# Attention beside linear attention on one core: a planner's fixed rules replaced by a table of rules per short stretch, and the last output rows summed ahead

## The chip, the cores and the metric

The kernel runs on one core of one Trainium2 chip. The metric is the device time of one execution in microseconds (us); a kernel's time is the median over its runs. Engines are named as the profile names them: PE (TensorE, matmuls), PEld (its weight loads), DVE (VectorE), ACT (ScalarE), POOL (GpSimd), SP (SyncE, which issues most of the DMAs).

## What is computed

Two independent blocks, each on an input of 2048 rows by 512 columns in bfloat16, with 32 heads of 16 columns. Their outputs stand side by side in the result.

```python
# A: linear attention
phi = lambda t: jnp.where(t > 0, t + 1, jnp.exp(t)) + 1e-6
pq, pk = phi(q), phi(k)
kv = jnp.einsum("bhsd,bhse->bhde", pk, v)
z = jnp.einsum("bhsd->bhd", pk)
num = jnp.einsum("bhqd,bhde->bhqe", pq, kv)
den = jnp.einsum("bhqd,bhd->bhq", pq, z)[..., None] + 1e-6
a = (num / den).transpose(...).reshape(B, S, D) @ wo
# B: full softmax attention
scores = jnp.einsum("bhqd,bhkd->bhqk", q, k) * Dh ** -0.5
p = softmax(scores, axis=-1)
b = jnp.einsum("bhqk,bhkd->bhqd", p, v).transpose(...).reshape(B, S, D) @ wo
out = jnp.concatenate([a, b], axis=-1)
```

B has 32 x 2048 x 2048 scores, so 134 million exponentials; A is small beside it.

## The kernel before, in words

**Tiling of B.** The heads go in four groups of eight (`Gp`), a group in two halves of four heads (`e_`), the queries in four chunks of 512 (`c`). One unit is one group, one chunk and one half: 32 units, each with 16 key tiles for each of 4 heads, so 64 blocks. A block is 128 keys by 512 queries of one head; there are 2048 of them. The four heads of a unit sit in four row strips of PE (32 rows each) when scores are made, and in four column strips (17 columns: 16 of V and one of ones, which sums the row) when probabilities are multiplied with V, so up to four blocks run side by side.

**Two ways through the exponential.** A block's scores (line 727, `qk`) go either into the PSUM tile `pS`, or into one of the two banks of `pD`.

- The ACT way: `pS` has two slots, of three banks and of two. When a slot is filled (`fill_act_cand`), ACT takes the exponential of all its blocks in one instruction (line 896, 128x1536 or 128x1024) and writes `PT`. One PV matmul per block follows (line 971, `pPV<-PT`).
- The DVE and POOL way: DVE turns one bank of scores into 16-bit integers whose bits are a power of two (line 808, `DI<-pD`), and POOL adds two shifts to a pair of such blocks (line 832), which gives three approximations that are summed with three scaled copies of V. So three PV matmuls per block follow (`pPV<-DI`). `fill_d_cand` and `d_pick` decide which block goes this way and when.

After a unit's last PV matmul `unit_done` (line 987) transposes `pPV` on DVE (line 991), takes the reciprocal of the row sums on DVE (996), multiplies on POOL (997), and after the second half transposes the result into `ON` on DVE (1002). In the last group each finished chunk yields four output jobs (`omm_job`, line 671): four matmuls with Wo (line 675), an eviction (450) and a store (679). Block A is cut into jobs too (K, V, their sum, Q, denominators, numerators, output), which use the banks of `pD`.

**What sets the order.** Nothing is written out by hand. When the program is built, a planner runs through the work with its own clock for each engine and, step by step, picks the next instruction among the candidates: a fill of a `pS` slot, a block for `pD`, one to three rounds of PV matmuls (`pv_cand`), a stage of a job. Each candidate has a start time and a priority, and of those that could start within 0.03 us of the earliest the best priority is taken. `lim` is the planner's latest time at which PE must be free for the next fill of a slot; longer candidates are put off. Constants steer it: `DEFER` and `FLOW` (how early a fill is urgent), `DPR` and `DDEL` (priority and delay of a `pD` block), `PVR`, `PVMIN`, `PVURG` (rounds of PV, how many must be ready), `DBL` and `DLEAD` (how much work may queue on DVE and POOL), `DNEXT`, `ALAG`, `SLK`. Every engine then executes its own instructions strictly in the planned order, and waits on semaphores for the others. So a heavy row in PE's list delays every fill behind it.

`filler` (line 1115) puts idle matmuls into PE's planned gaps: into `pPV` with weights of zero (1125) or into a free bank of `pD` with the identity (1134). They change no result.

Of the kernel before, what the change touches and what calls it, by code (L numbers as in the profile page):

```python
# [231 lines left out]
def bass_concat_heads__linear_attn_block__softmax_full_mha__prompt_kernel(nc, A_x, A_wqkv, A_wo, B_x, B_wqkv, B_wo, out):  # L232
# [15 lines left out]
    DNEXT = 16  # L248
    DEND = 20
    TEND = 720.0  # L250
    ALAG = 10.0
    DLEAD = 1.0
    DBL = 3.0
    TRACE = None

# [6 lines left out]
    with es:  # L262
# [140 lines left out]
        class Job:  # L403
# [11 lines left out]
            def stage_done(self, i, end, bk, bi):  # L415
                if i == self.rel and bi is not None:
                    jfree[bi] = end + LAT
                for st, tk in self.gives:
                    if st == i:
                        tok[tk] = end + LAT  # L420
                if i + 1 < len(self.stages):
                    eng, dur, fn = self.stages[i + 1]
                    lat = LAT if eng != self.stages[i][0] else 0.0
                    push(eng, end + lat, self.prio if eng == "pe" else (0 if i + 1 <= self.rel and self.bank else min(self.prio, 2)), dur,
                         lambda st_, en_, fn=fn: (fn(bk), self.stage_done(i + 1, en_, bk, bi)), "PORT" in getattr(fn, "keys", ()))
# [11 lines left out]

        MM, TRB = 0.2155, 0.0555
# [4 lines left out]
        SLK = 0.0  # L443
        FMARG = 0.06
        DEFER, FLOW, DPR, DDEL = 0.15, 3.5, 4.2, 0
        PVR, PVMIN, PVURG = 3, 4, 32
# [237 lines left out]

        rem = [[list(range(NT)) for g in range(4)] for u in range(NU)]
# [30 lines left out]
        def take(bl, parts):  # L716
            for u, j, g in bl:
                rem[u][g].remove(j)
                pv_all[u][g] += parts
                left[u] -= 1  # L720
                if left[u] == 0 and (u + 1) % (NC * 2) == 0:
                    tok[("filled", u // (NC * 2))] = T["pe"]

# [38 lines left out]
        def d_pick(at, used):  # L762

            u = cur_unit()
            bi = min((i for i in range(2) if jfree[i] is not None), key=lambda i: (jfree[i], i), default=None)
            if bi is None or jfree[bi] > at or not d_open() or d_backlog(at) > DBL:
                return None
            if (ajobs and at > ajobs[0].ready + ALAG) or (bjobs and at > bjobs[0].ready + ALAG and bjobs[0].start_time() is not None):
                return None
            if u < NU - 1 and left[u] < DNEXT:  # L770
# [133 lines left out]
        def fill_d_cand():  # L904
            fr = [x for x in jfree[0:2] if x is not None]
            if not fr:
                return None
            busy = max(T["dve"], T["pe"]) + sum(c_[3] for c_ in cands["dve"] if c_[0] < T["dve"] + 1.0)
            at = max(T["pe"], min(fr), busy - DLEAD, T["pe"] + d_backlog(T["pe"]) - DBL + 0.01)
# [12 lines left out]
            return at, QK, run  # L922
# [4 lines left out]
        def pv_cand(lim, short):  # L927
# [20 lines left out]
            for R in range(1, PVR + 1):  # L948
# [7 lines left out]
            if n < (PVMIN if lim is not None else 4) and not final and not (short and n >= 1):  # L956
                return None
# [27 lines left out]
            return t_, dur, run, (1 if out_ >= PVURG or final else 4)  # L985

        def unit_done(u, t_):
# [7 lines left out]
            zr = ZR[:, 0, 0:16]  # L995
            st = [("dve", 0.25, f_op("dve", lambda e: e.reciprocal(zr, o[:, :, 16]), [("OT", 0)], [("ZR", 0)])),  # L996
                  ("pool", 0.65, f_op("pool", lambda e: e.tensor_tensor(xn[:, :, 16 * e_:16 * e_ + 16], o[:, :, 0:16],  # L997
# [77 lines left out]
        def job_cand():  # L1075
# [7 lines left out]
            for lst, pr in ((urgent, 0.5), (early, 2), (bjobs, 2.2), (urgent2, 2.3), (ajobs, 2.5)):  # L1083
                for pos, j_ in enumerate(lst[:1] if lst is not urgent2 else lst[:8]):
# [9 lines left out]
                    if best is None or (st, pr) < (best[0], best[1]):  # L1094
                        def run(st_, en_, j_=j_, lst=lst, fn=fn):
# [4 lines left out]
                            fn(bk)  # L1100
                            j_.stage_done(0, en_, bk, b_)
                        best = (st, pr, eng, dur, run)
# [41 lines left out]
        npick = 0  # L1144
        while True:
            opts = []
            for eng in T:
# [6 lines left out]
                if best is not None:  # L1154
                    c_ = best[2]
                    opts.append(pe_opt(best[1], c_[1], c_[3], c_[4], c_, "f") if eng == "pe" else (best[1], c_[1], eng, c_[3], c_[4], c_))
            fa = fill_act_cand()
            if fa is not None:
                lim = max(T["act"] + sum(exps) - fa[1] - PH - LAT - SLK, fa[0]) if nfill[0] >= 2 else None
                have = sum(x is not None and x <= fa[0] + 0.05 for x in jfree[0:2])  # L1160
                want = min(2, 4 - ABL[nfill[0] % 2])
                fao = pe_opt(fa[0], 0 if lim is None or fa[0] + DEFER > lim or have >= want or not d_open() else FLOW, fa[1], fa[2], None, "q")
                opts.append(fao)
            fd = fill_d_cand()
            if fd is not None:
                opts.append(pe_opt(fd[0] + DDEL, DPR, fd[1], fd[2], None, "q"))
            elif not d_open():
                close_group()
            if fa is None or nfill[0] < 2:
                lim = None  # L1170
            pc = pv_cand(lim, fa is None and not cands["act"])
            if pc is not None:
                opts.append(pe_opt(pc[0], pc[3], pc[1], pc[2], None, "v"))
            jc = job_cand()
            if jc is not None:
                opts.append(pe_opt(jc[0], jc[1], jc[3], jc[4], None, "f") if jc[2] == "pe" else (jc[0], jc[1], jc[2], jc[3], jc[4], None))
# [3 lines left out]
            if lim is not None:  # L1180
                keep = [o for o in opts if o[2] != "pe" or o is fao or o[0] + o[3] <= lim or o[0] + 1e-9 < fa[0] - o[3]]
                opts = keep
            t0 = min(o[0] for o in opts)
            o = min((o for o in opts if o[0] <= t0 + 0.03), key=lambda o: (o[1], o[0]))
# [99 lines left out]
```

## Time and profile before

| what | value |
|---|---|
| time, median of 3 runs | 738.66 us (735.14 to 738.72) |
| the profiled execution | 740.72 us, of which 738.8 us lie between its first and last instruction (the span) |
| granted TensorE clock, mean | 0.988 |
| instructions | 15635 |
| weight loads (PEld) | 229.5 us busy |
| bytes moved | 17.33 MB, most of it in the first 37 us |
| last exponential ends, span ends | 723.57 us, 738.8 us |

In the profile's rows a group gives its busy time and the mean length of one instruction; where instructions of an engine overlap, the mean is longer than the distance from one to the next. In rows of waits and in square brackets of a timeline, the engine and line behind the arrow is what ended the idle time. Granted clock 1.00 is full speed, 0.50 half.

### The profile page before, as it was taken

How to read it: one execution, taken by the hardware profiler on the slowest of the kernel's cores; microseconds unless marked ns; L12 is line 12 of the kernel's file. 1: busy time of each engine (PE TensorE's matmuls, PEld its weight loads, DVE VectorE, ACT ScalarE, POOL GpSimd, SP SyncE). 2: the span in 40 equal slices, each digit the busy share in tenths (PEclk: the TensorE clock that was granted, in tenths of full speed). 3: DMA queues.
4: the chain of work that ended last, by engine and by line, in shares of the span. 5: the costliest groups of instructions: out<-in, count | busy, mean ns of one | idle time of the engine just before them, and what ended most of it. 6: DMA issues, size and time to landing. Idle time of an engine off the chain costs nothing.

```text
span 738.8 us, 15635 instructions
## 1 busy us (share of the span) xinstructions
PE 694.7 (94%) x6677; PEld 229.5 (31%) x6677; DVE 519.3 (70%) x918; ACT 704.7 (95%) x657; POOL 535.0 (72%) x325
## 2 busy tenths in 40 slices
PE   7999999999999999999999999999999999999986
PEld 4333433333333333322222232222222222222221
DVE  5878656576666776678786778867777767776751
ACT  6899999898999999999999999999999999989992
POOL 4596446566876776767898869867788867879780
PEclk9999999999999999999999999999999989999998
DMA  9800000000000000100100000000100001010001
GB/s 212 216 2 2 2 1 10 8 12 5 1 2 1 2 1 2 36 8 12 34 16 15 2 8 23 24 19 11 23 16 23 8 17 28 22 44 8 30 1 32
DMA packets 35788, 17.33 MB, mean 23 GB/s; under 512 B 26496, under 2 KB 35200, under 8 KB 35712
## 3 DMA queue, kind: packets, MB, share of 16 engines
q1 hardware_dynamic: 34912, 15.87, 8.7%
q8 instruction: 54, 0.88, 0.5%
q10 hardware_dynamic: 800, 0.39, 0.2%
q14 instruction: 22, 0.18, 0.1%
HBM read 4.72 MB, written 4.19 MB: 12 GB/s over the span
## 4 chain that ended last, share of the span: by engine, by line
ACT 77%; PE 17%; DVE 2%; POOL 1%; DMA 1%; SPq 1%; issue 1%; DVEq 0%
ACT PT L896 75%; PE pPV L971 6%; PE pS L727 4%; ACT EA L586 2%; POOL DI L832 1%; PE pD L675 1%; PE pD L482 1%; DVE DI L808 1%; PE pD L566 1%; PE pD L597 1%; DMA xTb<-in_B_x_dram 1%; PE pD L727 1%; PE pD L1134 1%; SPq L344 1%; PE pD L622 0%
## 5 line engine op out<-in xcount | busy, mean ns | idle before, releaser
L896 ACT ACTIVATE PT<-pS 128x1536 f16<-128x1536 f32 x602 | 692.4, 1336 | 14.4 <-PE pD L727 11.1
L832 POOL TENSOR_TENSOR DI<-DI,SHC 128x1024 int32<-128x1024 int32 x272 | 509.7, 1891 | 174.2 <-DVE DI L808 148.0
L808 DVE TENSOR_SCALAR DI<-pD 128x512 int16<-128x512 f32 x539 | 359.8, 689 | 122.1 <-PE pD L727 114.2
L727 PE MATMUL pS<-QT,KM 32*128 32x512 bf16 x1504 | 235.3, 387 | 22.6 <-ACT PT L896 18.7
L971 PE MATMUL pPV<-PT,VV 128*17 128x512 f16 x1504 | 251.0, 386 | 1.1 <-ACT PT L896 0.8
L971 PE MATMUL pPV<-DI,VV 128*17 128x512 f16 x1632 | 243.5, 387 | 2.2 <-DVE OT L991 1.8
L727 PE MATMUL pD<-QT,KM 32*128 32x512 bf16 x544 | 194.6, 387 | 5.8 <-DVE DI L808 3.5
L727 PEld LDWEIGHTS pS<-QT,KM 32*128 32x128 bf16 x1504 | 57.2, 91 | 221.1 <-ACT PT L896 168.8
L971 PEld LDWEIGHTS pPV<-DI,VV 128*17 128x17 bf16 x1632 | 52.5, 88 | 75.3 <-issue 55.3
L971 PEld LDWEIGHTS pPV<-PT,VV 128*17 128x17 bf16 x1504 | 54.6, 88 | 61.9 <-issue 46.2
L727 PEld LDWEIGHTS pD<-QT,KM 32*128 32x128 bf16 x544 | 46.5, 91 | 58.3 <-DVE DI L808 31.2
L597 PE MATMUL pD<-Wa,xTa 128*128 128x128 bf16 x512 | 37.4, 220 | 1.0 <-DVE DI L808 0.6
L482 PE MATMUL pD<-xTb,Wb 128*128 128x512 bf16 x124 | 34.0, 384 | 0.9 <-DMA xTb<-in_B_x_dram 0.7
L991 DVE STREAM_TRANSPOSE OT<-pPV 128x512 f32<-128x512 f32 x32 | 22.8, 711 | 15.2 <-PE pPV L971 14.8
L597 PEld LDWEIGHTS pD<-Wa,xTa 128*128 128x128 bf16 x512 | 28.7, 98 | 14.3 <-DVE DI L808 7.3
L997 POOL TENSOR_TENSOR OT<-OT,ZR 128x256 bf16<-128x256 f32 x32 | 19.8, 620 | 16.3 <-DVE ZR L996 15.0
L586 ACT ACTIVATE EA<-pD 128x256 bf16<-128x256 f32 (+1 forms) x48 | 26.1, 544 | 0.0
L587 DVE TENSOR_SCALAR EA<-EA 128x256 bf16<-128x256 bf16 (+1 forms) x48 | 11.8, 245 | 18.5 <-POOL DI L832 8.4
L566 PE MATMUL pD<-Wb,xTb 128*128 128x128 bf16 x256 | 17.9, 220 | 1.8 <-DVE KM L495 0.7
L622 PE MATMUL pD<-xTa,Wa 128*128 128x512 bf16 x64 | 19.2, 398 | 0.1
L675 PE MATMUL pD<-WOa,ONT 128*128 128x512 bf16 x64 | 18.5, 383 | 0.1
L571 DVE CAST VV<-pD 128x512 bf16<-128x512 f32 x16 | 11.0, 689 | 8.2 <-PE pD L566 8.2
(89 smaller groups left out, 277.4 us busy)
## 6 DMA issues: line engine op xcount, KB each, us to landing
out_dram<-OB SPq DMA_DIRECT2D x16, 128.0 KB, 1.7
out_dram<-KNa SPq DMA_DIRECT2D x16, 128.0 KB, 1.8
Wa<-in_A_wqkv_dram SPq DMA_DIRECT2D x1, 1536.0 KB, 7.3
KM<-KR SPq DMA_DIRECT2D x96, 16.0 KB, 1.8
Wb<-in_B_wqkv_dram SPq DMA_DIRECT2D x2, 384.0 KB, 4.9
Wb<-in_B_wqkv_dram SPq DMA_DIRECT2D x1, 512.0 KB, 4.7
WOa<-in_A_wo_dram SPq DMA_DIRECT2D x1, 512.0 KB, 8.0
VNa<-in_B_wo_dram SPq DMA_DIRECT2D x1, 512.0 KB, 3.3
```

The costliest lines, as they stand in the source:

```text
L482: return e.matmul(f32v(bk), lhsT=Wb[:, cc, kind * 512 + Gp * 128:kind * 512 + Gp * 128 + 128], rhs=xTb[:, cc, sc * 512:(sc + 1) * 512], st ...
L566: return e.matmul(f32v(bk)[:, tl * 128:(tl + 1) * 128], lhsT=xTb[:, cc, t * 128:(t + 1) * 128], rhs=Wb[:, cc, 1024 + Gp * 128:1024 + Gp * ...
L586: ("act", 0.051 + n * 0.000833, f_ev("act", lambda e, bk: e.activation(EA[:, q, 0:n], f32v(bk)[:, c0:c0 + n], ACTF.Exp), [], [("EA", q)])),
L597: return e.matmul(f32v(bk)[:, 128 * x:128 * x + 128], lhsT=xTa[:, cc, (t + i_) * 128:(t + i_ + 1) * 128], rhs=Wa[:, cc, c0:c0 + 128], star ...
L675: return e.matmul(f32v(bk), lhsT=src, rhs=WO[:, hb, :], start=(hb == 0), stop=(hb == 3))
L727: return e.matmul(dst, lhsT=KM[32 * g:32 * g + 32, Gp % 2, e_, j * 128:(j + 1) * 128], rhs=QT[32 * g:32 * g + 32, Gp % 2, c * 512:(c + 1) ...
L808: sch.add("dve", lambda e: e.tensor_scalar(DI[:, buf, 0, i * 512:(i + n) * 512], DB[:, bi * 512:(bi + n) * 512], ESC, EB, op0=ALU.mult, op ...
L832: sch.add("pool", lambda e: e.tensor_tensor(DI32[:, buf, 1:3, 0:w], DI32[:, buf, 0, 0:w].unsqueeze(1).broadcast_to([128, 2, w]), SHC32[:]. ...
L896: sch.add("act", lambda e: e.activation(PT[:, row, c0:c0 + w], SCR[sl][:, 0:w], ACTF.Exp, scale=SC), reads=skeys(sl), writes=[("PT", row, ...
L971: sch.add("pe", lambda e, g=g, vk=vk, c0=c0, P=P, first=first, last_=last_: e.matmul(PVb[32 * g:32 * g + 17, 0:512], lhsT=VV[:, Gp % 2, vk ...
L991: sch.add("dve", lambda e: e.transpose(OT[:, 0, :], PVb[:, 0:512]), reads=[("PV", g) for g in range(4)], writes=[("OT", 0)])
L997: ("pool", 0.65, f_op("pool", lambda e: e.tensor_tensor(xn[:, :, 16 * e_:16 * e_ + 16], o[:, :, 0:16], zr.unsqueeze(2).broadcast_to([128, ...
```

## The change

**The rules come from a table.** The constants move into a table `POLICY` of 88 rows; row n holds while PE's planned clock is between 8n and 8(n+1) us, the last one to the end. A row has the old constants and four new numbers: `PA` and `PB` (added to the priority of PV and of jobs while the three-bank slot, or the two-bank slot, is next), `SEED` (a seed for random shifts of up to 0.7 in the priorities of PE's less urgent candidates) and `PARTS` (how many PE stages of one job may run in one piece, if they end before `lim`). `lim` is now also set while a slot is still held by its exponential. The rows were chosen by a search with the planner's own clock. In the diff the table is cut to two rows.

**The end.** Of the last four output row tiles, three of four Wo products are summed ahead (`pre_job`) once the last scores are filled; when the last chunk is finished one matmul per tile is left (`last_job`), and its eviction and store go to DVE and SP for two tiles, to ACT and ACT's own DMA queue for the other two. The multiply of the very last unit moves from POOL to DVE. After the last fill, `filler` uses half of a gap.

```diff
+    NAMES = ('DEFER', 'FLOW', 'DPR', 'DDEL', 'PVR', 'PVMIN', 'PVURG', 'DBL', 'DLEAD', 'DNEXT', 'ALAG', 'SLK', 'PA', 'PB', 'SEED', 'PARTS')
+    SEG = 8.0
+    POLICY = [
+        (0.15, 3.5, 4.2, 0, 3, 4, 32, 3.0, 1.0, 16, 10.0, 0.0, 0, 0, 0, 1),
...
+        (0.15, 3.5, 4.2, 0, 3, 4, 32, 3.0, 0.2, 16, 10.0, 0.0, 0, 0, 443, 2),
+    ]
...
-        DEFER, FLOW, DPR, DDEL = 0.15, 3.5, 4.2, 0
-        PVR, PVMIN, PVURG = 3, 4, 32
...
+        def pre_job(tl):
+            t = 12 + tl
+            def mm(bk):
+                prebank[tl] = bk
+                def f(e):
+                    for hb in range(3):
+                        ins = e.matmul(f32v(bk), lhsT=ON[:, 4 * hb + 3, tl * 128:(tl + 1) * 128], rhs=WOb[:, hb, :], start=(hb == 0), stop=False)
+                    return ins
...
+            return Job([("pe", 3 * MM, mm)], [("akv", 3), "lastfill"], [(0, ("pre", tl))], rel=99)
+
+        def last_job(tl, lane):
+            t, o2 = 12 + tl, 1 + tl
+            def mm(_):
+                bk = prebank[tl]
+                sch.add("pe", lambda e: e.matmul(f32v(bk), lhsT=ON[:, 15, tl * 128:(tl + 1) * 128], rhs=WOb[:, 3, :], start=False, stop=True),
...
+                stores.append(sch.add(out_lanes[o2], lambda e: e.dma_start(out[0][t * 128:(t + 1) * 128, 512:1024], obf(o2)),
+                                      reads=obk(o2), queue="sp" if lane == "dve" else "act", force_signal=True))
...
+            ml = "pool" if u < NU - 1 else "dve"
...
-                fin = u == NU - 1
                 for tl in range(4):
-                    ln = ("dve", "act")[tl % 2] if fin else "dve"
-                    urgent2.append(omm_job("b", 4 * c + tl, 1 + tl, [("on", Gp, c)], [(1, ("st", c, tl))], lane=ln))
+                    if u < NU - 1:
+                        urgent2.append(omm_job("b", 4 * c + tl, 1 + tl, [("on", Gp, c)], [(1, ("st", c, tl))]))
+                    else:
+                        urgent.append(last_job(tl, ("dve", "act")[tl % 2]))
...
+            if left[NU - 1] == 0:
+                gap *= 0.5
...
+            k_ = min(int(T["pe"] / SEG), len(POLICY) - 1)
+            if k_ != seg[0]:
+                seg[0] = k_
+                P.update(zip(NAMES, POLICY[k_]))
+                rng = random.Random(P["SEED"])
...
-                lim = max(T["act"] + sum(exps) - fa[1] - PH - LAT - SLK, fa[0]) if nfill[0] >= 2 else None
...
+                    lim = max(T["act"] + sum(exps) - QK - PH - LAT - P["SLK"], fa[0])
+                elif exps and afree[nfill[0] % 2] is None:
+                    lim = max(T["act"] + sum(exps) - QK - PH - LAT - P["SLK"], T["act"] + exps[0] + LAT)
...
+                near = [(o[0], o[1] + (rng.uniform(-0.7, 0.7) if o[2] == "pe" and o[1] > 1 else 0.0)) + o[2:] for o in near]
```

**What moves, counted over the whole lists.** The same instructions for jobs stand in both lists. Of the 2048 blocks 1504 went the ACT way before and 1477 do now; 544 and 571 go by DVE and POOL. ACT has 301 exponentials of three blocks, 300 of two and one of one before; now 295 and 296. DVE has 534 conversions of one block and 5 of two before, now 569 and 1. POOL has 272 shifts of a pair before, now 285 and one of a single block. PV matmuls are 1504 from `PT` and 1632 from `DI` before, now 1477 and 1713. Idle matmuls fall from 54 in `pPV` and 13 in `pD` to 27 and none. PE's PV matmuls wait for POOL in 216 rows before and in 246 now.

Three places follow. The first is PE's list early in the program, from the fill of one slot (`pS1`) to the next fills; `L566` and `L482` are projections of V and of Q and K there, `L971` is PV. Before:

```order
L727 MATMUL pS1<-QT,KM 128x512 x2
L482 MATMUL pD<-xTb,Wb 128x512 x2
L566 MATMUL pD<-Wb,xTb 128x128 x16
L971 MATMUL pPV<-PT,VV 17x512 x6
L971 MATMUL pPV<-DI,VV 17x512
L971 MATMUL pPV<-PT,VV 17x512 x2
L971 MATMUL pPV<-DI,VV 17x512 x2
L971 MATMUL pPV<-PT,VV 17x512
L727 MATMUL pS0<-QT,KM 128x512 x3
```

The same place in the changed kernel, whose line 862 is `qk`, 588 the projection and 1106 PV:

```order
L1106 MATMUL pPV<-PT,VV 17x512 x4
L862 MATMUL pS1<-QT,KM 128x512 x2
L588 MATMUL pD<-xTb,Wb 128x512 x2
L862 MATMUL pS0<-QT,KM 128x512 x3
L862 MATMUL pD<-QT,KM 128x512
L1106 MATMUL pPV<-PT,VV 17x512 x2
L1106 MATMUL pPV<-DI,VV 17x512
L1106 MATMUL pPV<-PT,VV 17x512 x2
L1106 MATMUL pPV<-DI,VV 17x512 x2
L1106 MATMUL pPV<-PT,VV 17x512
L862 MATMUL pS1<-QT,KM 128x512 x2
```

Before, 18 projection matmuls and 12 of PV stand between the two fills; now two of a projection stand there, and the 16 others and the PV come behind later fills. Three places of before have such a stretch on which the prediction rests; the second is 15 rows further on (six projection matmuls of 512 columns and 12 of PV between two fills), the third is here, late in PE's list, where three output jobs (`L675`) stand in one piece. Before:

```order
L727 MATMUL pS1<-QT,KM 128x512 x2
L727 MATMUL pD<-QT,KM 128x512
L675 MATMUL pD<-VNa,ON 128x512 x12
L647 MATMUL pD<-RHA,PQT 128x128 x4
L971 MATMUL pPV<-PT,VV 17x512 x3
L971 MATMUL pPV<-DI,VV 17x512 x3
L971 MATMUL pPV<-PT,VV 17x512
L971 MATMUL pPV<-DI,VV 17x512
L727 MATMUL pS0<-QT,KM 128x512 x3
```

The output jobs of the same chunk in the changed kernel (line 781):

```order
L781 MATMUL pD<-VNa,ON 128x512 x2
L862 MATMUL pS1<-QT,KM 128x512 x2
L862 MATMUL pD<-QT,KM 128x512
L781 MATMUL pD<-VNa,ON 128x512 x2
L862 MATMUL pS0<-QT,KM 128x512 x3
L781 MATMUL pD<-VNa,ON 128x512 x4
L862 MATMUL pS1<-QT,KM 128x512 x2
```

Halves of output jobs, at most four matmuls, now stand between fills, where twelve stood in one piece. Last, the end of PE's list. Before:

```order
L971 MATMUL pPV<-PT,VV 17x512 x3
L1125 MATMUL pPV<-identb,ZW 32x512
L971 MATMUL pPV<-PT,VV 17x512 x4
L1134 MATMUL pD<-identb 128x512 x12
L675 MATMUL pD<-VNa,ON 128x512 x8
L675 MATMUL pS0<-VNa,ON 128x512 x8
```

And in the changed kernel, whose lines 799 and 808 are `pre_job` and `last_job`:

```order
L862 MATMUL pS0<-QT,KM 128x512 x2
L799 MATMUL pD<-VNa,ON 128x512 x3
L1106 MATMUL pPV<-PT,VV 17x512 x7
L799 MATMUL pD<-VNa,ON 128x512 x3
L1106 MATMUL pPV<-PT,VV 17x512 x2
L799 MATMUL pS1<-VNa,ON 128x512 x6
L808 MATMUL pD<-VNa,ON 128x512 x2
L808 MATMUL pS1<-VNa,ON 128x512 x2
```

The 12 idle matmuls are gone, 12 of the 16 Wo products stand ahead of or among the last PV matmuls and right behind them, and four are left for the end.

More of the change, by code (lines that the diff above doesn't have):

```diff
@@ L1 @@
 import contextlib
+import random
 import struct
@@ L423, in stage_done, with chain, run_chain @@
                     lat = LAT if eng != self.stages[i][0] else 0.0
[L424 to L425 removed]
+                    if eng == "pe":
+                        push(eng, end + lat, self.prio, self.chain(i + 1), lambda st_, en_, n_=1: self.run_chain(i + 1, n_, en_, bk, bi))
+                    else:
+                        push(eng, end + lat, 0 if i + 1 <= self.rel and self.bank else min(self.prio, 2), dur,
+                             lambda st_, en_, fn=fn: (fn(bk), self.stage_done(i + 1, en_, bk, bi)), "PORT" in getattr(fn, "keys", ()))
+            def chain(self, i):
+                res = []
+                while i < len(self.stages) and self.stages[i][0] == "pe":
+                    res.append(self.stages[i][1])
+                    i += 1
+                return res
+            def run_chain(self, i, n_, en_, bk, bi):
+                for x in range(n_):
+                    self.stages[i + x][2](bk)
+                    if x + 1 < n_:
+                        for st, tk in self.gives:
+                            if st == i + x:
+                                tok[tk] = en_ + LAT
+                self.stage_done(i + n_ - 1, en_, bk, bi)
         def f_pe(fn, reads):
@@ L436, in f_op @@
             return op
+        P = dict(zip(NAMES, POLICY[0]))
         MM, TRB = 0.2155, 0.0555
@@ L722, in take @@
                     tok[("filled", u // (NC * 2))] = T["pe"]
+                    if u == NU - 1:
+                        tok["lastfill"] = T["pe"]
+                        urgent2.extend(pre_job(tl) for tl in range(4))
         def qk(e, dst, b):
@@ L947, in pv_cand @@
             best = None
-            for R in range(1, PVR + 1):
+            for R in range(1, P["PVR"] + 1):
                 n = sum(min(R, len(v_)) for v_ in byg.values())
```

72 lines of the change are left out of this document (45 added, 27 removed), and 86 rows, old and new, of the table POLICY.

## The prediction

> **What bounds the kernel now.** I read the page's busy times first, then the table by stretches, ACT's waits, and the timeline at the gaps and at the end.
>
> ```profile
> PE 694.7 (94%) x6677; PEld 229.5 (31%) x6677; DVE 519.3 (70%) x918; ACT 704.7 (95%) x657; POOL 535.0 (72%) x325
> ```
>
> ACT and PE are both almost always busy, so the averages alone don't say which one sets the time. A table of two stretches does:
>
> ```profile
> 100.00:150.00 50.00, 47.47 (x450) 17.38 (x448) 30.69 (x67) 47.66 (x47) 25.18 (x15) 0.97 0.03 7
> 350.00:400.00 50.00, 47.66 (x442) 13.51 (x436) 39.03 (x64) 50.00 (x46) 45.40 (x27) 1.00 0.10 24
> ```
>
> The columns behind the length are PE, PEld, DVE, ACT and POOL, then the clock. From 350 to 400 ACT is busy for all of the 50.00 us, while PE has 2.34 us left and POOL 4.60. ACT is the bound there. From 100 to 150 ACT loses 2.34 us. What it waits for in the whole run:
>
> ```profile
> ACT PT L896 <- PE pD L727: 11.1, 16, 2.3
> ACT PT L896 <- PE pS L727: 3.0, 7, 0.6
> ```
>
> So 11.1 + 3.0 = 14.1 us of waits before exponentials, by 23 waits, each for a fill that PE brought late. Three of them stand out in the timeline:
>
> ```profile
> 20.50 1.45 ACT L896 ACTIVATE PT<-pS 128x1536 f16<-128x1536 f32 x1 [1.20 <-PE pD L727]
> 26.27 1.45 ACT L896 ACTIVATE PT<-pS 128x1536 f16<-128x1536 f32 x1 [1.14 <-PE pD L727]
> 654.64 1.45 ACT L896 ACTIVATE PT<-pS 128x1536 f16<-128x1536 f32 x1 [2.30 <-PE pD L727]
> ```
>
> 1.20 + 1.14 + 2.30 = 4.64 us, a third of the waits. The square bracket is ACT's idle time. In the order these are the three heavy stretches shown above: between two fills PE has 18 projection and 12 PV matmuls, then 6 and 12, then 12 of an output projection in one piece.
>
> The time is therefore: ACT's work, plus 14.1 us in which PE is late, plus a start, plus an end in which ACT has nothing to do. The end:
>
> ```profile
> 711.58 11.99 ACT L896 ACTIVATE PT<-pS 128x1024 f16<-128x1024 f32 x11
> 724.99 5.34 PE L1134 MATMUL pD<-identb 128*128 128x512 bf16 x12
> 725.10 0.72 DVE L991 STREAM_TRANSPOSE OT<-pPV 128x512 f32<-128x512 f32 x1 [11.89 <-PE pPV L971]
> 725.85 0.25 DVE L996 RECIPROCAL ZR<-OT 128x16 f32<-128x16 f32 x1
> 726.18 0.62 POOL L997 TENSOR_TENSOR OT<-OT,ZR 128x256 bf16<-128x256 f32 x1 [8.67 <-DVE ZR L996]
> 726.83 0.71 DVE L1002 STREAM_TRANSPOSE ON<-OT 128x512 bf16<-128x512 bf16 x1 [0.73 <-POOL OT L997]
> 730.38 1.90 PE L675 MATMUL pD<-VNa,ON 128*128 128x512 bf16 x8
> 732.12 1.89 PE L675 MATMUL pS<-VNa,ON 128*128 128x512 bf16 x8
> 732.32 0.60 ACT L450 ACTIVATE KNa<-pD 128x512 bf16<-128x512 f32 x1 [8.75 <-PE pD L675]
> 733.19 0.69 DVE L450 CAST KNa<-pS 128x512 bf16<-128x512 f32 x1 [1.03 <-PE pS L675]
> 734.05 0.60 ACT L450 ACTIVATE KNa<-pS 128x512 bf16<-128x512 f32 x1 [1.13 <-PE pS L675]
> ```
>
> The exponentials end at 711.58 + 11.99 = 723.57. `ON` is complete at 726.83 + 0.71 = 727.54, but PE is in its 12 idle matmuls until 724.99 + 5.34 = 730.33 and starts the projection at 730.38: 2.84 us late. The last eviction ends at 734.65, and 4.15 us of stores and ending follow to 738.8.
>
> **The change part by part. First, blocks leave ACT.** 27 of 1504 blocks move. In a stretch without a gap the chain of work shows:
>
> ```profile
> 516.06 65.54 ACT PT L896 x58
> ```
>
> 58 exponentials of 2.5 blocks on average take 65.54 us, so 65.54 / (58 x 2.5) = 0.452 us per block, and 27 x 0.452 = 12.2 us less on ACT. Since ACT is the bound, this is on the path, as long as DVE, POOL and PE take the blocks up:
>
> ```profile
> L832 POOL TENSOR_TENSOR DI<-DI,SHC 128x1024 int32<-128x1024 int32 x272 | 509.7, 1891 | 174.2 <-DVE DI L808 148.0 <-DVE EA L587 15.6 <-DVE VV L575 9.4
> L808 DVE TENSOR_SCALAR DI<-pD 128x512 int16<-128x512 f32 x534 | 353.7, 684 | 118.9 <-PE pD L727 110.9 <-issue 2.4 <-PE pS L727 1.9
> L808 DVE TENSOR_SCALAR DI<-pD 128x1024 int16<-128x1024 f32 x5 | 6.1, 1225 | 3.2 <-PE pD L727 3.2
> L971 PE MATMUL pPV<-PT,VV 128*17 128x512 f16 x1504 | 251.0, 386 | 1.1 <-ACT PT L896 0.8
> L971 PE MATMUL pPV<-DI,VV 128*17 128x512 f16 x1632 | 243.5, 387 | 2.2 <-DVE OT L991 1.8
> L727 PE MATMUL pS<-QT,KM 32*128 32x512 bf16 x1504 | 235.3, 387 | 22.6 <-ACT PT L896 18.7
> L727 PE MATMUL pD<-QT,KM 32*128 32x512 bf16 x544 | 194.6, 387 | 5.8 <-DVE DI L808 3.5 <-DVE VNa L601 0.9 <-DVE PQT L589 0.2
> L1125 PE MATMUL pPV<-identb,ZW 128*32 128x512 bf16 x54 | 15.7, 390 | 0.0
> L1134 PE MATMUL pD<-identb 128*128 128x512 bf16 x13 | 5.1, 390 | 0.7
> ```
>
> POOL: 13 more pairs at 1.891, half a pair more, and 0.62 less: 24.6 + 0.9 - 0.6, so 535.0 becomes 560. DVE: 35 x 0.684 - 4 x 1.225 = 19.0, so 519.3 becomes 538. Both stay under 80% of 717 us. PE: 81 more PV at 243.5 / 1632 = 0.149 is 12.1; 27 fewer at 251.0 / 1504 = 0.167 is -4.5; scores -27 x 0.156 + 27 x 0.358 = +5.5; idle matmuls -27 x 0.291 - 5.1 = -13.0. The sum is +0.1: PE's real work grows, but the idle matmuls that go make room for it. Moving blocks to `pD` is hidden by DVE's and POOL's free quarter; were that cover gone, it is the slower rival below.
>
> **Second, PE's order between fills.** The three heavy stretches are gone in the new list, so I take away their 4.64 us. The other 9.5 us of waits I leave as they are. A count over the two lists speaks for fewer: at 1.90 / 8 = 0.24 us for a matmul of 512 columns or a round of four PV (the rows of `L675` above) and a quarter of it for 128 columns, and without the very last stretch, 8 stretches between two fills hold over 1.5 us of PE's work before and 3 now, the heaviest 3.57 before and 1.71 now. But each list meets waits for DVE and POOL that the count leaves out, and the trace can't show those of the new one. Bounds: nearly all of them go (-9.5 more), or new ones of the size of the three come back and the same again (+9.3, by 4.64 twice). I take zero, nearest to the 20 small waits that are there already.
>
> **Third, the end.** Steps up to the last PV matmul stay. The multiply on DVE has no row; bounds are the same shape in another DVE operation, and a pass of twice the width at 0.69 (the eviction above):
>
> ```profile
> L589 DVE SCALAR_TENSOR_TENSOR KNa<-pD,EA 128x256 bf16<-128x256 f32 x32 | 13.6, 424 | 1.0
> 0.80 0.49 ACTq L331 DMA_DIRECT2D ON<-in_B_x_dram  x1
> ```
>
> I take 0.42. It replaces 0.62 and a hop of 0.08 to POOL, so `ON` comes 0.25 earlier: 723.57 + 3.72 in the old time. PE is free then: the six sums behind its last PV take 6 x 0.24 = 1.4 us (1.90 / 8 each), and DVE needs 2.2 from the same point. Four matmuls remain. DVE evicts tiles 0 and 2, ACT 1 and 3. ACT's first starts some 0.75 after `ON` (a hop, two matmuls of 0.24, their way out), takes 0.60, then ACT issues its own store, 0.49 by the row above, and evicts again, 0.60 and a hop: the last eviction ends 3.72 + 0.75 + 0.60 + 0.49 + 0.60 + 0.05 = 6.2 after the exponentials, where it ended 11.1 after. That is 4.9 us less. The ending of 4.15 stays; the last store now comes from ACT's queue, which I cost at no difference. Bounds 3.5 (half clock, a slow queue) to 6.0 (the store's issue doesn't hold ACT).
>
> **Fourth, idle matmuls and the clock.**
>
> ```profile
> 130.00:135.00 5.00, 4.23 (x34) 1.15 (x30) 4.34 (x9) 4.13 (x5) 2.79 (x2) 0.90 0.09 21
> 135.00:140.00 5.00, 5.00 (x45) 1.31 (x37) 2.37 (x5) 4.02 (x4) 4.39 (x4) 0.76 0.00 0
> 140.00:145.00 5.00, 4.79 (x63) 2.34 (x60) 2.87 (x6) 4.62 (x6) 2.41 (x2) 1.00 0.01 3
> 720.00:725.00 5.00, 4.37 (x26) 1.02 (x23) 0.00 (x0) 3.57 (x4) 0.00 (x0) 0.66 0.00 0
> ```
>
> From 130 on the clock falls (0.90, 0.76), and ACT loses 0.87 + 0.98 + 0.38 = 2.23 us in these 15 us: PE at half clock cannot keep up. The mean clock of 0.988 says that this was rare. I leave its number as it is, since PE's real work replaces the idle matmuls.
>
> By the Trainium skill, page "TensorE: Matmul & The Clock Gate", Part 1, the clock is halved after an idle stretch of a free-running window of about 3.4 us, and sustained work restores it. That speaks against taking idle matmuls out, and by it the last four matmuls could run cold, an estimated 4 x 0.24 = 1.0 us more at the end. The trace agrees only in part: PE was busy for 4.23 of the 5.00 us in which the clock began to fall, so it need not be idle for a whole window.
>
> **The sum.** 738.8 - 12.2 - 4.6 - 4.9 = 717.1 us of span. The profiled execution took 740.72, 1.92 more than its span, and the median of the runs is 738.66; I carry the difference of 21.7 over to the median: 738.66 - 21.7 = 717.0 us.
>
> **The rivals.**
>
> - *PE becomes the bound.* With 694.8 us of work in 717 it would be busy 96.9%; from 350 to 400, with ACT never idle, it was busy 47.66 / 50 = 95.3%. If that is its ceiling, the span is 694.8 / 0.953 = 729 us. For it: PE's 14.1 us of lateness. Against: those 2.34 idle us were waits for ACT. Somewhere between, 722 to 730.
> - *The clock falls more often.* From a few stretches to six more, at 2.2 us each: 717 + 13 = 730. It decides when the mean granted clock drops under some 0.97. This is where the Trainium skill's page on the clock gate would lead.
> - *The order gains more.* Most of the remaining 9.5 us go too: 708 to 712.
> - *Slower: POOL cannot follow.* PE waits in its list for POOL's shifts in 246 places, and every fill behind such a wait is late. If POOL, which waits for pairs from DVE, could not be busy for more than 75% on average, 560 / 0.75 = 747 us. It turns slower than before by over 0.5% from 560 / 742.4 = 75.4% down. For it: 174.2 us of idle time before the shifts, 72% now. Against: 45.40 of 50 from 350 to 400.
> - *Little comes of it.* Gains are given back by new gaps of 18 us or more: 735 to 742.
>
> **How the numbers follow.** Forecast (712 to 722) 0.45; PE bound 0.20; clock 0.08; order gains more 0.14; little 0.06; slower 0.07. The range of 709 to 730 holds the first, the second, and most of the third and fourth, some 0.80. Half a per cent, 3.7 us, is about what a measurement of this kernel can tell from no change, as its three runs lie 3.6 apart. Faster by more: 0.45 + 0.20 + 0.08 + 0.14 = 0.87; within 0.06; slower 0.07.
>
> **What would show it.** Right: ACT's busy time near 692.5, its waits before exponentials near 9.5 us, none at the three places; the time from the last exponential to the end near 10.3 us in place of 15.2, and no idle matmuls there. Wrong: waits of ACT over 20 us, POOL or DVE named as what PE waits for before fills, a mean clock under 0.97, or an end that is no shorter because PE or a store is late.

## The result, and the profile after

The changed kernel takes 714.82 us (median of 4 runs, 710.88 to 714.86), the kernel before 737.19 us beside it. The ratio is 0.9685, 95% interval 0.964 to 0.973. The forecast was 717.0, in a range of 709 to 730. The profiled execution took 714.82 us with a span of 713.1 (before: 740.72 and 738.8). So the two profiles lie 25.9 us apart and the medians 22.4: the profile of before is one of its slower executions. Beside the later experiments one execution of the kernel before took 3010.64 us; it is in no ratio.

The page's busy times of the changed kernel:

```profile
PE 672.3 (94%) x6691; PEld 223.7 (31%) x6691; DVE 537.0 (75%) x950; ACT 691.8 (97%) x646; POOL 559.2 (78%) x338
```

ACT is down by 12.9 us, DVE up by 17.7 and POOL by 24.2, as the counts of blocks said. PE is down by 22.4 with 14 matmuls more; its share of the span stayed at 94%. So the page's busy PE goes with the span here and does not measure PE's work. The same stretch of 50 us as before, and one around 190 us:

```profile
190.00:195.00 5.00, 4.64 (x28) 1.02 (x28) 3.81 (x8) 4.61 (x5) 4.96 (x3) 0.69 0.00 0
195.00:200.00 5.00, 5.00 (x48) 2.35 (x49) 3.32 (x9) 3.86 (x4) 2.95 (x4) 0.62 0.01 2
350.00:400.00 50.00, 47.49 (x484) 13.30 (x482) 41.49 (x68) 50.00 (x45) 47.72 (x29) 1.00 0.09 22
```

From 350 to 400 ACT is still never idle, with POOL now at 47.72. At 190 the clock is at 0.69 and 0.62, and ACT loses 0.39 + 1.14 us. ACT's waits before exponentials and its last rows show the two parts that shrank:

```profile
ACT PT L1031 <- PE pD L862: 2.2, 5, 1.0
ACT PT L1031 <- PE pS L862: 1.6, 4, 0.8
ACT PT L1031 <- issue: 0.4, 1, 0.4
```

The waits are 2.2 + 1.6 + 0.4 = 4.2 us where they were 14.1, and none is at the three places. The end of the changed kernel, in order of time:

```profile
702.51 1.35 ACT L1031 ACTIVATE PT<-pS 128x1024 f16<-128x1024 f32 x1
704.87 0.72 DVE L1126 STREAM_TRANSPOSE OT<-pPV 128x512 f32<-128x512 f32 x1 [10.83 <-PE pPV L1106]
705.91 0.42 DVE L1133 TENSOR_TENSOR OT<-OT,ZR 128x256 bf16<-128x256 f32 x1
706.37 0.71 DVE L1138 STREAM_TRANSPOSE ON<-OT 128x512 bf16<-128x512 bf16 x1
707.14 0.60 PE L808 MATMUL pD<-VNa,ON 128*128 128x512 bf16 x2 [0.91 <-DVE ON L1138]
707.78 0.60 ACT L556 ACTIVATE KNa<-pD 128x512 bf16<-128x512 f32 x1 [3.93 <-PE pD L808]
708.41 0.37 ACTq L813 DMA_DIRECT2D out_dram<-KNa  x1
708.89 0.60 ACT L556 ACTIVATE KNa<-pS 128x512 bf16<-128x512 f32 x1 [0.51 <-ACT KNa L556]
```

The last exponential ends at 703.86. The Wo product starts 0.06 us after `ON` is complete, where it was 2.84 late, and the last eviction ends at 709.49, 5.63 after the exponentials (11.08 before). The span ends 9.24 after them (15.23 before).

One part worked against the change in this execution: the start. In each kernel's timeline, the first projection and the first exponential; before:

```profile
6.28 1.04 PE L482 MATMUL pS<-xTb,Wb 128*128 128x512 bf16 x4 [0.73 <-ACT xTb L450]
9.41 3.71 ACT L896 ACTIVATE PT<-pS 128x1536 f16<-128x1536 f32 x3 [0.60 <-PE pS L727]
```

And after:

```profile
7.15 1.89 PE L588 MATMUL pS<-xTb,Wb 128*128 128x512 bf16 x4 [0.69 <-ACT xTb L556]
12.18 2.37 ACT L1031 ACTIVATE PT<-pS 128x1536 f16<-128x1536 f32 x2 [0.80 <-PE pS L862]
```

The instructions up to there are the same. Four matmuls took 1.04 us in one execution and 1.89 in the other, so PE ran at about half speed, and the exponentials began 2.77 us later. The views' clock column says 1.00 there, because a trace's clock records begin only when full clock comes: at 4.3 us in the profile of before, at 11.0 us in this one. So the spans differ by +2.8 at the start, 691.68 - 714.16 = -22.5 between the first exponential and the last (of it 9.9 are waits, the other 12.6 ACT's work), and -6.0 at the end: -25.7 in all.

### The profile page after: what moved, and what is told of

Read it like the earlier page. It is cut to its first block, busy times and chain, and to the rows that moved or that the text cites. A ratio compares the mean times of both kernels' runs of the same rounds, so it can differ in the third digit from the quotient of the medians.

```text
span 713.1 us, 15692 instructions
## 1 busy us (share of the span) xinstructions
PE 672.3 (94%) x6691; PEld 223.7 (31%) x6691; DVE 537.0 (75%) x950; ACT 691.8 (97%) x646; POOL 559.2 (78%) x338
## 4 chain that ended last, share of the span: by engine, by line
ACT 78%; PE 12%; POOL 6%; DVE 3%; issue 1%; DVEq 0%; POOLq 0%; ACTq 0%
ACT PT L1031 76%; POOL DI L967 5%; PE pPV L1106 3%; PE pS L862 3%; ACT EA L692 2%; DVE DI L943 1%; PE pD L703 1%; PE pD L862 1%; PE pD L588 1%; PE pD L781 1%; DVE KNa L695 0%; PE pD L1151 0%; PE pD L672 0%; DVE EA L693 0%; DVE VNa L707 0%
## 5 line engine op out<-in xcount | busy, mean ns | idle before, releaser
L1031 ACT ACTIVATE PT<-pS 128x1536 f16<-128x1536 f32 (+1 forms) x591 | 680.1, 1345 | 4.8 <-PE pD L862 2.2
L967 POOL TENSOR_TENSOR DI<-DI,SHC 128x1024 int32<-128x1024 int32 (+1 forms) x286 | 534.3, 1888 | 129.3 <-DVE DI L943 86.9
L943 DVE TENSOR_SCALAR DI<-pD 128x512 int16<-128x512 f32 x570 | 377.2, 685 | 95.5 <-PE pD L862 84.9
L1106 PE MATMUL pPV<-DI,VV 128*17 128x512 f16 x1713 | 247.7, 382 | 1.8 <-DVE OT L1126 1.6
L862 PE MATMUL pS<-QT,KM 32*128 32x512 bf16 x1477 | 231.2, 386 | 19.0 <-ACT PT L1031 13.8
L1106 PE MATMUL pPV<-PT,VV 128*17 128x512 f16 x1477 | 248.0, 384 | 1.1 <-ACT PT L1031 1.0
L862 PE MATMUL pD<-QT,KM 32*128 32x512 bf16 x571 | 206.3, 386 | 7.3 <-DVE DI L943 2.5
L862 PEld LDWEIGHTS pS<-QT,KM 32*128 32x128 bf16 x1477 | 56.3, 91 | 213.2 <-ACT PT L1031 164.4
L1106 PEld LDWEIGHTS pPV<-PT,VV 128*17 128x17 bf16 x1477 | 53.0, 88 | 66.9 <-issue 51.3
L862 PEld LDWEIGHTS pD<-QT,KM 32*128 32x128 bf16 x571 | 49.7, 91 | 62.7 <-DVE DI L943 34.3
L728 PE MATMUL pD<-xTa,Wa 128*128 128x512 bf16 x64 | 17.6, 383 | 0.3 <-DVE DI L943 0.2
```

The source lines that it names most:

```text
L862: return e.matmul(dst, lhsT=KM[32 * g:32 * g + 32, Gp % 2, e_, j * 128:(j + 1) * 128], rhs=QT[32 * g:32 * g + 32, Gp % 2, c * 512:(c + 1) ...
L943: sch.add("dve", lambda e: e.tensor_scalar(DI[:, buf, 0, i * 512:(i + n) * 512], DB[:, bi * 512:(bi + n) * 512], ESC, EB, op0=ALU.mult, op ...
L967: sch.add("pool", lambda e: e.tensor_tensor(DI32[:, buf, 1:3, 0:w], DI32[:, buf, 0, 0:w].unsqueeze(1).broadcast_to([128, 2, w]), SHC32[:]. ...
L1031: sch.add("act", lambda e: e.activation(PT[:, row, c0:c0 + w], SCR[sl][:, 0:w], ACTF.Exp, scale=SC), reads=skeys(sl), writes=[("PT", row, ...
L1106: sch.add("pe", lambda e, g=g, vk=vk, c0=c0, P=P, first=first, last_=last_: e.matmul(PVb[32 * g:32 * g + 17, 0:512], lhsT=VV[:, Gp % 2, vk ...
```

## The experiments

Times are medians; the ratio is to the kernel before, run beside it on the same chip.

**Old end.** The changed kernel with the end of before.

```diff
-                        urgent2.extend(pre_job(tl) for tl in range(4))
+                        pass
...
-            ml = "pool" if u < NU - 1 else "dve"
+            ml = "pool"
...
-                        urgent.append(last_job(tl, ("dve", "act")[tl % 2]))
+                    ln = ("dve", "act")[tl % 2] if u == NU - 1 else "dve"
+                    urgent2.append(omm_job("b", 4 * c + tl, 1 + tl, [("on", Gp, c)], [(1, ("st", c, tl))], lane=ln))
...
-                gap *= 0.5
```

> The changed kernel with the old end (no products summed ahead, the last multiply on POOL, idle matmuls in whole gaps); everything before the last fill stands as in the changed kernel. If blocks, waits and end add up as independent terms: last exponential to the end 15 us in place of 9.2, so 714.8 + 6 = 721 us, with the exponentials ending at the same place. Rival: the old end was long because PE ran at half clock there, and at full clock it is only 13: 718 to 719 us.

718.11 us, ratio 0.975 (0.9715 to 0.9785). Its timeline's end:

```profile
700.35 1.35 ACT L1031 ACTIVATE PT<-pS 128x1024 f16<-128x1024 f32 x1
702.07 5.34 PE L1272 MATMUL pD<-identb 128*128 128x512 bf16 x12
703.92 0.71 DVE L1138 STREAM_TRANSPOSE ON<-OT 128x512 bf16<-128x512 bf16 x1 [0.73 <-POOL OT L1133]
711.14 0.60 ACT L556 ACTIVATE KNa<-pS 128x512 bf16<-128x512 f32 x1 [1.56 <-PE pS L781]
```

The exponentials end at 701.70 and the span at 715.2: 13.5 us, not 15.2. The rival's time holds: the new end is worth 13.5 - 9.2 = 4.3 us between these two profiles (3.3 between the medians, 4.8 by the ratios). Its cause, half clock, covers 1.0 of the other 1.7: the last eviction ends 10.04 us after the exponentials here and 11.08 in the profile of before, whose last PV matmuls ran in the stretch with 0.66. The other 0.7 lie behind that eviction (3.46 us to the span's end, 4.15 before), where PE has nothing left to do. The idle matmuls again end 2.8 us after `ON` (702.07 + 5.34 = 707.41 against 704.63).

**New end alone.** The kernel before with `pre_job`, `last_job`, the multiply on DVE and the half gap, all as in the diff of the change.

> The kernel before with the new end alone; 1504 blocks still go by ACT and the three heavy stretches stay. If the terms are independent: 5 to 6 us under the kernel before, ratio 0.992 to 0.993, ACT's waits before exponentials still 9 to 15 us and its idle times at the same three places. Rival: the new end only pays with the new order, because its sums ahead come in the way of the last PV: 0 to 3 us, ratio 0.996 to 1.0.

732.8 us, ratio 0.9947 (0.9927 to 0.9968): 3.9 us by the ratio, 4.6 between the medians, a little under the 5 to 6 expected and near the 4.3 of the run above. The exponentials end 11.2 us before the span does, 1.9 more than in the changed kernel: the last PV matmuls end later here, and the first eviction on ACT starts 5.00 us after the exponentials in place of 3.92. ACT's waits:

```profile
ACT PT L925 <- PE pD L756: 9.2, 10, 2.3
ACT PT L925 <- PE pS L756: 1.7, 4, 0.7
```

10.9 us with the order of before, 3.2 less than in its own profile; the three places are there with 1.14, 1.14 and 2.30. So some 3 us of the 14.1 were not the order's, as far as one profile of each can say. Two stretches show where they lie. In the profile of before:

```profile
130.00:145.00 15.00, 14.02 (x131) 4.80 (x127) 9.58 (x19) 12.76 (x13) 9.60 (x6) 0.89 0.03 8
590.00:602.00 12.00, 12.00 (x88) 2.52 (x84) 7.70 (x14) 10.57 (x11) 7.38 (x5) 0.72 0.00 1
```

And in this one:

```profile
130.00:145.00 15.00, 13.73 (x143) 5.28 (x143) 9.57 (x20) 13.88 (x14) 9.67 (x7) 1.00 0.04 10
590.00:602.00 12.00, 11.43 (x101) 3.22 (x102) 9.46 (x17) 12.00 (x13) 9.09 (x6) 1.00 0.04 13
```

At full clock ACT loses 1.12 us from 130 to 145 in place of 2.24, and nothing from 590 to 602 in place of 1.43. With 0.5 us at the first exponentials that is nearly all of the 3.2. The half of the loss at 130 to 145 that stays belongs to the order.

**The 27 blocks' work back on ACT.** The order stays, 27 exponentials of one block are added.

```diff
+                    nexp[0] += 1
+                    if nexp[0] % 22 == 11:
+                        sch.add("act", lambda e: e.activation(XS[:], SCR[sl][:, 0:512], ACTF.Exp, scale=SC),
+                                reads=skeys(sl), writes=["XS"])
```

> The changed kernel, its order untouched, with 27 more exponentials of one block (512 columns) on ACT, one ahead of every 22nd exponential, into a tile that nobody reads: the ACT work of the 27 blocks that moved, and nothing else. If ACT is the bound all along: 27 x 0.45 to 0.50 = 12 to 13.5 us more, 727 to 728 us. Rival (PE has become the bound, so that ACT has room): 5 us or less, under 720 us, with the idle time of PE before fills unchanged.

725.73 us, ratio 0.9851 (0.9808 to 0.9893), 10.9 us more than the changed kernel, and by the ratios (0.9851 - 0.9685) x 737 = 12.2. ACT's busy time rose by 12.8 to 704.6, 0.474 per block; its waits were 3.8. Nearly all of it comes through: ACT is still the bound, and the blocks that moved are worth some 12 us.

**Room on PE.** The order stays, 120 idle matmuls more on PE.

```diff
+                if npv[0] % 4 == 0 and not (left[u] == 0 and pv_cnt[u] == pv_all[u]):
+                    sch.add("pe", lambda e, g=g: e.matmul(PVb[32 * g:32 * g + 32, 0:512], lhsT=ZW[:],
...
+                            reads=["ZW", "identb"], writes=[("PV", g)], accum=("pv", u, g))
```

> The changed kernel, its order untouched, with 120 more idle matmuls of 512 columns with zero weights, one behind every fourth group of PV matmuls: 120 x 0.22 = 26 us more on PE, nothing else. If ACT is the bound and PE has room before fills (164.4 us of its weight loads waited for ACT): 0 to 4 us more, 715 to 719 us, ACT's waits up by as much. Rival (PE at 94% is as good as the bound): over half of the 26 us come through, 728 us or more.

716.32 us, ratio 0.9708 (0.9673 to 0.9742): some 2 us for 120 matmuls more. The 26 us are an upper estimate of their work, since they use one column strip and may run beside other matmuls; the page's busy PE rose by 13.2, to 685.5, and 2 us are little of that too. The profile fell on the slowest of the four executions (720.5 us, the others 714.5 to 716.4): in it PE's weight loads waited 141.6 us for ACT in place of 164.4, and ACT's waits rose to 6.0 + 1.8 + 0.4. PE at 94% was not the bound.

**Room on POOL.** The order stays, a memset follows each of the 286 shifts.

```diff
+                sch.add("pool", lambda e: e.memset(PX[:], 0.0), writes=["PX"])
```

> The changed kernel, its order untouched, with one idle memset of 0.2 us on POOL behind each of the 286 shifts: 57 us more on POOL (559 to 616 of 713), nothing else. If POOL still has room: 0 to 4 us more, under 719 us. Rival (POOL at 78% is close to setting the time, since PE waits for it in its list): over half of the 57 us come through, 740 us or more.

722.61 us, ratio 0.981 (0.977 to 0.985), 8 us more. Neither bound is met: the memsets take 58.7 us by their row, POOL's busy time rises by 40.1 to 599.3 since some overlap the shifts, and a fifth of that comes through. ACT's waits rise to 5.5 + 4.1 and its own busy time by 2.6, to 694.4. PE's waits for POOL rise too:

```profile
PEld pPV L1108 <- POOL DI L968: 12.3, 26, 2.0
```

In the changed kernel this row has 3.9 us. So POOL has room, but not for all of this work.

**Shifted seeds.** Every seed of the table is one higher.

```diff
-                rng = random.Random(P["SEED"])
+                rng = random.Random(P["SEED"] + 1)
```

> The changed kernel with every seed of the table raised by one; rules and code are the same. Its order has 1499 blocks on ACT (1477 in the changed kernel, 1504 before) and 12 stretches between fills with over 1.5 us of PE's work (3 and 8), the heaviest 4.27. Theory (the time follows blocks on ACT and heavy stretches): 22 x 0.452 = 10 us of ACT's work and at least 6 us of waits come back, 730 to 736 us, near the kernel before with the new end. Rival (the kinds of rules carry the gain, whatever the seeds): 714 to 720 us.

749.25 us, ratio 1.0185 (1.0132 to 1.0238): slower than before, and by more than the theory gave. Its waits:

```profile
ACT PT L1031 <- PE pD L862: 20.1, 23, 2.8
ACT PT L1031 <- PE pS L862: 3.7, 7, 1.1
ACT EA L692 <- PE pD L703: 2.2, 2, 1.7
```

26.0 us, 22 more than in the changed kernel, and 22 x 0.474 = 10.4 us of ACT's work: 714.8 + 32.2 = 747. The direction of the theory holds, its time of 730 to 736 us does not: "at least 6 us" of waits were 22. The rival falls: with these seeds the rules carry nothing.

**No random shifts.** With the sizes of that miss, the count of heavy stretches was put to a number (the 1.2 us were chosen then, with three orders known) and tried on a new order.

```diff
-            if P["SEED"]:
+            if False:
```

> The changed kernel with the random shifts of priorities off; the other rules of the table stay. Its order has 1500 blocks on ACT. Summing PE's work over 1.2 us in all stretches between fills gives 7.4 us for the order of before (10.6 to 14.7 us of waits in the profiles), 2.1 for the changed one (3.9 to 4.7), 17.5 for the one with shifted seeds (26.2), and 11.0 here. Theory (time follows ACT's blocks and this sum): 15 to 18 us of waits, 23 x 0.473 = 11 us of ACT's work back, so 714.8 + 11 + 12 = 738 us, 735 to 742, no gain over the kernel before. Rival (the rules without the shifts do most of it): under 725 us.

742.98 us, ratio 1.008 (1.0052 to 1.0109).

```profile
ACT PT L1031 <- PE pD L862: 11.6, 20, 1.5
ACT PT L1031 <- PE pS L862: 6.3, 11, 1.2
```

17.9 us of waits, as expected at the upper end of 15 to 18, and a time 1 us over the expected range; its end took 11.7 us after the last exponential where the changed kernel's took 9.2. The four orders side by side; the 26.0 hold 2.2 us before exponentials of block A:

| order | blocks on ACT | PE's work over 1.2 us between fills | ACT's waits | time |
|---|---|---|---|---|
| changed | 1477 | 2.1 us | 4.2 us | 714.8 us |
| before | 1504 | 7.4 us | 14.1 us (10.9 with the new end) | 737.2 us |
| no random shifts | 1500 | 11.0 us | 17.9 us | 743.0 us |
| seeds plus one | 1499 | 17.5 us | 26.0 us | 749.3 us |

**No idle matmuls**, in the changed kernel and in the one before; `filler` returns at once in both.

```diff
         def filler(gap):
+            return
```

> The changed kernel without its 27 idle matmuls; all else in the same order. If PE's real work alone keeps the clock up: 714 to 716 us, no more than one or two half-clock stretches between 15 and 700 us. Rival (idle matmuls hold the clock, as the Trainium skill's page on the clock gate would have it): five or more half-clock stretches at 1 to 2 us of ACT's waits each, 720 us or more.

716.84 us, ratio 0.9722 (0.9689 to 0.9755), all four runs between 716.5 and 717.1. The clock in three stretches of its profile:

```profile
190.00:200.00 10.00, 9.78 (x82) 3.46 (x86) 6.25 (x13) 8.21 (x8) 8.00 (x5) 0.66 0.00 1
425.00:440.00 15.00, 14.26 (x118) 3.66 (x115) 11.11 (x21) 13.74 (x13) 13.43 (x8) 0.77 0.00 0
695.00:710.00 15.00, 12.36 (x67) 2.93 (x67) 2.70 (x5) 9.20 (x10) 3.08 (x3) 0.77 0.01 1
```

Three stretches, one more than expected and fewer than the rival's five. The profiles of the same order with its idle matmuls have one to three such stretches too, so their number does not tell the two apart. The one at 695 falls into the end, which takes 11.0 us here in place of 9.2. The 27 are worth about 2 us by the medians, which the intervals of the two ratios do not tell from nothing.

> The kernel before without its 67 idle matmuls; all else in the same order. At the end the projection no longer stands behind 12 of them: 2.8 us less there, if the clock stays up. Elsewhere as for the changed kernel: 734 to 736 us with the clock as it was, or 742 us and more if the 54 others held it.

738.03 us, ratio 1.0006 (0.9983 to 1.003): no gain, a miss. Its timeline at the end:

```profile
729.71 2.83 PE L675 MATMUL pD<-VNa,ON 128*128 128x512 bf16 x8 [2.55 <-DVE ON L1002]
732.33 2.69 PE L675 MATMUL pS<-VNa,ON 128*128 128x512 bf16 x8
```

The projection starts 4.05 us after the last exponential (725.66) in place of 6.81, so 2.8 earlier, but its 16 matmuls now take 5.3 us in place of 3.6: PE had been idle for 2.55, and the clock is 0.66 from 730 to 735:

```profile
730.00:735.00 5.00, 5.00 (x16) 1.74 (x14) 1.39 (x2) 0.60 (x1) 0.00 (x0) 0.66 0.18 57
```

So a part of the 2.8 is lost again. The whole end still takes 12.4 us in place of 15.2; in this pair of profiles the gain goes elsewhere, as the last exponential ends 2.1 us later (the first begins 1.1 later, and ACT's waits are 10.5 + 4.3 = 14.8 in place of 14.1). That the idle matmuls paid by holding the clock is not shown: between the first and the last exponential both profiles have four half-clock stretches. Shown is that leaving them out alone gains nothing that can be measured.

**A fuller start and another store.** First, 33 in place of 28 idle matmuls on a tile that is ready sooner, and 6 more ahead of the first projection:

```diff
-            for i_ in range(28):
-                ins = e.matmul(f32v(DBANK[0], 128), lhsT=identb[:], rhs=identb[:], start=True, stop=True)
+            for i_ in range(33):
+                ins = e.matmul(f32v(DBANK[0], 128), lhsT=WT[:], rhs=WT[:], start=True, stop=True)
...
+        sch.add("pe", warm2, reads=["WT"], writes=[DBANK[0][3]])
```

> The changed kernel with more idle matmuls ahead of the first scores: 33 in place of 28, on a tile that is ready earlier, and 6 between the first transposes and the first projection, where PE waits for ACT; the order behind stays. First exponentials began at 9.4 to 12.2 us in the profiles so far, late where full clock came at 10.8 or 11.0, early where it came at 4.3 to 6.3. If the clock's window decides and the 6 matmuls fill it, the first exponential always begins at 9.4 to 10.4, and the median falls by 0 to 3 us, to 712 to 714, with less spread between runs. Rival (the loads decide): no change in the spread, 714.8 us.

713.72 us, ratio 0.9679 (0.9652 to 0.9707). Then with the second tile's store on SP as well, and the changed kernel beside it:

```diff
-                                      reads=obk(o2), queue="sp" if lane == "dve" else "act", force_signal=True))
+                                      reads=obk(o2), queue="act" if tl == 3 else "sp", force_signal=True))
```

> The changed kernel with the fuller start (more idle matmuls before the first scores), and with the store of the second of the last four tiles issued by SP, so that ACT evicts the fourth tile without issuing a store first: last eviction 5.1 us after the last exponential in place of 5.63, 0.3 to 0.5 us less at the end; with 0 to 3 us at the start: 711 to 714 us. Rival: the third store on SP queues and the end stays as it was, 713 to 715.

> The changed kernel once more, beside the version with the fuller start: 711 to 715 us, the first exponential at 9.4 to 10.4 or at 12.2 us as the clock's window falls.

712.73 us, ratio 0.967 (0.9638 to 0.9701), and 714.17, ratio 0.9694 (0.9663 to 0.9726). The two cannot be told apart by time, nor the first version (713.72) from either. The store does what it should in the trace of that version:

```profile
697.69 5.86 ACT L1033 ACTIVATE PT<-pS 128x1536 f16<-128x1536 f32 x5
707.48 0.60 ACT L558 ACTIVATE KNa<-pD 128x512 bf16<-128x512 f32 x1 [3.93 <-PE pD L810]
707.97 0.59 ACT L558 ACTIVATE KNa<-pS 128x512 bf16<-128x512 f32 x1
```

ACT's second eviction ends at 708.56, 5.0 after the last exponential, 0.6 earlier than in the changed kernel, and the span ends 8.8 us after it in place of 9.2. The start: over all fourteen profiles of this case the first exponential goes with the time at which full clock comes, the first of a trace's clock records. Where that was 4.2 to 5.6 us it began at 9.4 to 10.0, where it was 6.1 to 7.0 at 10.3 to 10.6, and at 10.8 and 11.0 at 12.1 and 12.2. The fuller start lies on the same line (9.63 and 10.38, with full clock at 4.2 and 6.1), so it brings nothing by itself; whether it makes the late case rarer stays open, since only two of the other twelve profiles had it. The runs spread as before (711.4 to 714.7).

## Why the prediction was right

- **Blocks off ACT: right.** Forecast 12.2 us; 12.6 by the profiles (12.9 of busy time), and 12 when the work was put back alone. The step that carried it, ACT as the bound, held where work was added: 12.8 us on ACT cost 10.9 to 12.2, while the matmuls added on PE cost 2.
- **Waits: right mechanism, too small.** The step said that the 4.64 us at three places go and the other 9.5 stay. The three went, but the waits fell by 9.9. Of the 5.3 too little, about 3 were no property of the order: with the same order and the new end the waits were 10.9. The prediction had one of their places in hand, the 2.23 us from 130 to 145, and put all of it down to the clock and none of it into the sum; half of it stays at full clock. The rest of the 5.3 is the order: the count of PE's work between fills spoke for fewer waits, and I set it aside for waits on DVE and POOL that did not come up. The two other orders agree with the count as a price, one of them ahead of its run.
- **The end: right in total, by luck in part.** Forecast -4.9, measured -6.0, and -4.3 against the old end in the new order. My sum started from PV matmuls at half clock, which the row with 0.66 showed and I carried along. The steps themselves came out: multiply on DVE 0.42 us (forecast 0.42), last eviction 5.63 after the last exponential (6.2). The 4.15 us behind it, which I left as they were, became 3.61.
- **The sum: close, with errors that cancel in part.** Without what was peculiar to the profile of before, the parts are 12 for the blocks, 10.9 - 4.2 = 6.7 for the waits and 4.3 for the end, 23 us in all, where the medians moved by 22.4. The forecast of 21.7 has 2 too little in the waits and 0.6 too much in the end.
- **The start was not in the sum.** It cost 2.8 us in the profile of after. That the same instructions start 9.4 or 12.2 us in is one reason why single executions of one kernel differ by 3 to 4 us.
- **Rivals.** PE as the bound: refuted, as 120 matmuls more cost 2 us. Its numbers were weak as well: the prices per matmul came from rows of groups that overlap (the six rows of matmuls in the prediction add up to 945 us, the page's busy PE is 694.7), so the sum of +0.1 could not be added to the page's figure, which fell by 22.4. The clock: there was one half-clock stretch between the first and the last exponential after, not six more. POOL unable to follow: it was busy 78%, above the 75% at which that rival ended, but the run with the memsets shows that the room is less than I thought when I put 0 to 4 us on it. As for the rival that little comes of it: the same code gives 749 us with other seeds and 743 without the shifts, so the gain hangs on this one list.

What stays open: why the clock falls at 190 to 194 us in six of the nine profiles of the changed order, and at 427 to 434 in five. The stretch at 190 alone holds 1.0 of the 4.2 us of waits before exponentials of B in the profile of after.

## What to carry to other kernels

Where one engine is the bound and others bring its work in order, add up two things from the order alone: the bound engine's instructions, and what the feeding engine has in one piece between two feedings beyond what the buffer covers. Here the second sum ranked four orders as the chip did, and the blocks on ACT told the changed order from the other three (1477 against 1499 to 1504), which they do not rank. And an order found by search is a single good point: keep its exact list, since neighbours with the same rules can be slower than the plain one.

## What the runs showed of the hardware

- The clock fell to half without a long idle time of PE: 4.53 of the 5.00 us before the stretch at 190 us were busy. What got fewer are the matmuls, 15 in the 3 us ahead of the fall after 28 in 2 us:

```profile
185.00:190.00 5.00, 4.53 (x54) 1.79 (x50) 3.65 (x7) 5.00 (x7) 4.36 (x4) 1.00 0.02 3
187.00:189.00 2.00, 2.00 (x28) 0.94 (x25) 1.16 (x2) 2.00 (x4) 2.00 (x2) 1.00 0.00 0
189.00:192.00 3.00, 2.44 (x15) 0.62 (x14) 2.68 (x7) 3.00 (x3) 2.55 (x3) 0.99 0.00 0
192.00:194.00 2.00, 2.00 (x14) 0.37 (x13) 1.37 (x3) 2.00 (x3) 2.00 (x2) 0.50 0.00 0
```

The Trainium skill, page "TensorE: Matmul & The Clock Gate", Part 1, ties half clock to an idle window. In the clock records of the fourteen traces the clock fell 28 times between the first and the last exponential, each time for 3.41 or 6.83 us. In the 3.41 us ahead PE was busy for 54% to 95% by the page's measure, and 14 to 25 matmuls started there in 26 of the 28 cases, where the median of all other such stretches is 32. So few matmuls go with the fall, but other stretches with as few did not bring it, and no run separates their number from their size (score matmuls use 32 of PE's rows).

- A store issued by ACT between two evictions held the second one back by 0.51 us (0.37 of it the issue itself), and none when SP issued it.
